# Linear attention and a gated convolution on one core: from four tokens of a head per partition to nine, with all transposes on TensorE and a new instruction list

## The chip, the core and the metric

The kernel runs on one core of a Trainium2 chip. The metric is the device time of one execution, in microseconds (us). Three executions of the kernel before took 235.14, 232.63 and 233.62 us, median 233.62.

## The reference

Two stages follow each other, for 8 batches of 576 tokens. The first is an attention without softmax over pairs, with 8 heads of 64 columns and 128 projected features:

```python
def phi(x):                                   # q and k alike
    proj = np.einsum('bhsd,df->bhsf', x, w_phi)
    proj = proj - np.max(np.abs(proj), axis=-1, keepdims=True)
    return np.concatenate([np.exp(proj), np.exp(-proj)], axis=-1)
kv  = np.einsum('bhsf,bhsd->bhfd', k_p, v)
num = np.einsum('bhsf,bhfd->bhsd', q_p, kv)
den = np.einsum('bhsf,bhf->bhs', q_p, z)[..., None] + 1e-06   # z: sum of k_p over the tokens
```

`num / den`, its heads side by side, is x (576 x 512 per batch). The second stage is a gated layer: `gate[s] = sigmoid(sum over k of conv_w[k] * x[s-4+k])`, five taps of its own for each of the 512 columns, then `(gate * (x @ w_val)) @ w_out`.

## The kernel before

**Units.** A partition holds four tokens that follow each other of each head, so 128 partitions hold 512 tokens of a head. The 64 tokens that are left over in each batch are a "tail". A pair of batches is worked off in nine units of 1024 rows each: one tail unit (two batches, eight heads, 64 tokens) and eight main units (one batch and one pair of heads each). There are 36 units. The head pair lies in the two halves of TensorE's rows.

**One unit, in the names of the instruction list.** `LD` loads and casts to bf16 (GpSimd's DMA queue). `T` transposes k and q on TensorE (L331: 8 whole-array transposes into one PSUM bank), `Tc` copies the bank to SBUF (L224 on VectorE, L222 on ScalarE). `PK` and `PQA` project with tokens on the partitions (L342: pairs of 64-row matmuls of 128 columns, one in each row half), only the largest absolute value of each row is wanted of the q one. `mKa`, `mK`, `mQa`, `mQ` are these row maxima on VectorE (L356, 128x512 each). `K0` to `K3` are the exponentials of k on ScalarE (L388, 128x512), `E` those of the maxima. k's shift is not subtracted but multiplied into v: `V` on GpSimd (L408, L412). `KV` sums over tokens (L445: 16 matmuls of 65 columns, and L450: 4 more for the tail's tokens, with zeroed rows for the other batch). `KVM` copies that sum to SBUF. `PQ` projects q a second time with the features on the partitions (L466: 2 matmuls of 512 columns), `SH` subtracts q's maxima in PSUM (L476: 8 whole-array matmuls of 128 columns, the maxima broadcast as the stationary operand, a negative identity as the moving one). `Qa`, `Q` are the exponentials of q (L484, four of 128x512). `NUM` multiplies with the k-v sum (L509; L523 for the tail), `XN` divides (L534, L536).

**From x to the output.** `XP` puts x's columns on the partitions, by DMA transposes that SyncE issues (L545 for the main tokens, L548 for tails) into `XT` and `XH`; `HL` copies a halo of four tokens. `GA` is the convolution: for each of five taps a diagonal matrix times shifted columns (L604: the array in four tiles of 64x64, 32 matmuls in one `GA`, two `GA` per batch). `TH` is the gate's tanh on ScalarE (L612, 128x1024), `VA` the value product (L617, 16 matmuls of 512 columns per batch), `GV` gate times value (L633), `OUT` the last product (L642), `OE` its copy (L649 on ScalarE, L651 on VectorE), `ST` the store (SyncE). `GAt` to `STt` do the same for tails (L673, L681, L704, L716).

**Order.** `ORDER` is one written list of these names. A number behind a name is the unit or the batch tile, `@` names PSUM banks, and the letter behind the colon an engine. The engines get their instructions in the list's order and wait for each other by semaphores. PSUM is eight banks of 512 float32 columns, allotted by the list. `GA`, `VA` and `OUT` of a batch stand between the attention ops of later batches.

Of the kernel before, what the change touches and what calls it, by code (L numbers as in the profile page):

```python
# [2 lines left out]

# [7 lines left out]
ALU = mybir.AluOpType  # L11
# [9 lines left out]
SM = 512  # L21
ST = S - SM
E1 = D + 1
PL = 144
TL = 80
NG = B // 2
NU = 9 * NG


# [3 lines left out]
LD7 LD6 CK0 CQ0 T1@1 LD2 ND0:A W20 Tc1:D PK1@2,5 mKa1 PQA1@6,1 K01 mK1 mQa1 mQ1 T0@0 LD0 Tc0:A  # L33
PQ1@3,4 PK0@7,6 K11 K21 mKa0 T2@0 E1 Tc2:D K31 K00 SH1 Qa1 LD1 PK2@1,0 mK0 mKa2 LD3 mK2 PQA2@3,5
mQa2 ZV0:P LD8 K20 mQ2 T3@2 E0 Tc3:D PQA0@3,5 mQa0 mQ0 K02 K10 K30 E2 K22 PK3@7,6 mKa3 PQA3@2,5
LD4 mQa3 Q1 LD9 PQ2@3,4 SH2 LD10 mK3 K32 K12 T4@0 Tc4:D PK4@1,0 K03 Qa2 mQ3 V0:P K23 V1:P KV1@3 Q2
LD5 V2:P mKa4 K33 K04 KVM1:D NUM1@4 PQ3@6,3 SH3 mK4 XN1 LD11 K13 KV2@2 K24 LD31 PQA4@7,4 KVM2:D E3
mQa4 K14 mQ4 PQ0@1,5 K34 SH0 LD30 Qa3 Qa0 NUM2@6 PQ4@2,0 T5@4 T6@1 Q3 SH4 Q0 XN2 Qa4 E4 Tc5:D
Tc6:D PK5@7,6 mKa5 K05 PQA5@3,1 PK6@2,5 mQa5 Q4 LD13 K15 mK5 LD12 V3:P K25 KV3@3 mQ5 V4:P mKa6 K06
LC0 K35 KVM3:D E5 V5:P LD32 LD39 PQ5@0,1 TP0@7 mK6 Vb0:P NUM3@3 CW0 XP1 XN3 K16 XP2 T7@7 Tc7:D K26  # L40
SH5 Qa5 PQA6@6,2 mQa6 PK7@3,7 mKa7 KV4@4 PQA7@6,0 mQ6 mQa7 XP3 K36 T8@5 Tc8:D mK7 PQ6@2,6 Q5
KVM4:A SH6 K07 NUM4@4 mQ7 XN4 E6 PK8@0,1 K17 mKa8 Qa6 K27 T9@2 Tc9:D Q6 XP4 PQA8@3,5 V6:P PQ7@4,6
SH7 mQa8 LD15 mK8 K08 K37 PQA9@2,3 mQ8 mQa9 KV5@7 KVM5:D mQ9 T10@5 Tc10:D K18 PQ8@0,2 SH8 Qa7
PK9@4,7 mKa9 T11@3 E7 V7:P Q7 PK10@5,6 Tc11:D K28 mKa10 LD14 DG0:P Qa8 K38 KV6@3 Q8 K09 NUM5@0 mK9
KVM6:D NUM6@2 XN5 K010 mK10 KV7@0 K29 K110 XN6 K19 KVM7:D T12@5 PK11@1,4 mKa11 K210 HL0:P Tc12:D
XP6 LD16 K39 GA0@2 K310 mK11 K011 NUM7@6 VAa1@0 LD40 XN7 E8 VAb1 TH0 GV1 V8:P PK12@2,5 PQA10@3,6
K111 PQ9@1,7 SH9 VAa2@0 K211 mQa10 mKa12 LD19 VAa0@3 mK12 E9 LD17 K311 Qa9 VAb0 mQ10 KV8@4 KVM8:D
VAb2 GV0 PQA11@1,6 K012 V9:P Q9 mQa11 K212 PQ10@4,7 SH10 mQ11 K112 T13@3 Tc13:D NUM8@1 XN8 E10
# [54 lines left out]

class _U:
    pass

@with_exitstack
def kernel(  # L110
# [30 lines left out]

    PS = psum.tile([P, 8, 512], FP32, name="PS")


    units = []
    for G in range(NG):
        for kind in range(9):
# [616 lines left out]
```

## Time and profile before

| | |
|---|---|
| three executions | 235.14, 232.63, 233.62 us, median 233.62 |
| span of the profiled execution | 232.5 us, 8372 instructions |
| that execution's own time | not recorded apart from its span; the median of the runs is 1.1 us above the span |
| busy: TensorE, VectorE, ScalarE, GpSimd | 205.8, 184.2, 188.6, 125.4 us |
| first matmul, first gate matmul, last matmul's end | 4.8, 56.1, 227.7 us |
| DMA | 62002 packets, 30.90 MB |

PE is TensorE's matmuls, PEld its weight loads (they overlap), DVE VectorE, ACT ScalarE, POOL GpSimd, SP SyncE. "Busy" counts from an instruction's start to its recorded end. Matmuls, and also instructions of the other engines, overlap their successors, so a share of the chain of work says better what an instruction costs in a sequence than its duration does.

### The profile page before, as it was taken

Reading aid. Unit: us, or ns where it says so; the run is one execution under the profiler, and the core shown is the slowest. Engines: PE = TensorE matmul, PEld = TensorE weight load, DVE = VectorE, ACT = ScalarE, POOL = GpSimd, SP = SyncE. Lnnn points to the kernel's source line nnn. Section 1 sums busy time; section 2 is a strip of 40 time slices with the busy share of each in tenths; the row PEclk is TensorE's granted clock in tenths of the full one; section 3 lists DMA queues with packets and bytes.
Section 4 is the critical chain, followed back from the end, with each engine's and each line's share of the span. In section 5 each row is a group of like instructions: output and inputs, shape, how many; then the busy total and the mean of one; then the engine's idle time right before and its main releaser. Section 6 shows DMA issues by size and latency. Waiting matters only on the chain.

```text
span 232.5 us, 8372 instructions
## 1 busy us (share of the span) xinstructions
PE 205.8 (89%) x3497; PEld 139.5 (60%) x3516; DVE 184.2 (79%) x335; ACT 188.6 (81%) x419; POOL 125.4 (54%) x142
## 2 busy tenths in 40 slices
PE   1286797888999989899999999999899999999991
PEld 1264675666666746567666766766476667564550
DVE  5559669999989979699999879897799788554451
ACT  3189869999997988599999979998899999934251
POOL 8909935999979437774919751564526241100000
PEclk9998579999999999999999999999999999999997
DMA  8997995979999942999994992499903928126195
GB/s 151 246 198 97 106 180 80 92 101 178 129 194 128 139 32 32 129 257 177 128 114 68 180 186 92 39 115 126 214 6 37 169 77 259 38 52 200 27 355 185
DMA packets 62002, 30.90 MB, mean 133 GB/s; under 512 B 33420, under 2 KB 59148, under 8 KB 61964
## 3 DMA queue, kind: packets, MB, share of 16 engines
q0 software_dynamic: 36144, 14.29, 58.2%
q1 hardware_dynamic: 25468, 15.78, 33.6%
q8 instruction: 27, 0.44, 0.8%
q10 hardware_dynamic: 352, 0.30, 0.4%
q14 instruction: 11, 0.09, 0.2%
HBM read 30.48 MB, written 9.44 MB: 172 GB/s over the span
## 4 chain that ended last, share of the span: by engine, by line
PE 69%; ACT 11%; DMA 9%; DVE 5%; issue 3%; SPq 1%; POOL 1%; POOLq 0%; DVEq 0%; ACTq 0%
PE PS L617 11%; PE PS L642 10%; PE PS L342 7%; PE PS L604 7%; PE PS L476 7%; PE PS L445 6%; PE PS L331 6%; DMA XT<-XN 6%; PE PS L509 5%; ACT QTIL L484 5%; ACT KTIL L388 3%; DMA kT<-in_k_dram 3%; PE PS L466 3%; PE PS L681 2%; DVE MQ L356 2%
## 5 line engine op out<-in xcount | busy, mean ns | idle before, releaser
L408 POOL TENSOR_TENSOR VT<-vN,E 128x1024 bf16<-128x1024 bf16 x27 | 51.5, 1907 | 60.4 <-issue 34.2
L388 ACT ACTIVATE KTIL<-PS 128x512 bf16<-128x512 f32 x128 | 76.7, 666 | 5.3 <-DVE MK L356 5.1
L484 ACT ACTIVATE QTIL<-PS 128x512 bf16<-128x512 f32 x128 | 71.0, 666 | 2.5 <-PE PS L476 1.1
L356 DVE TENSOR_REDUCE MK<-PS 128x4 f32<-128x512 f32 x72 | 47.9, 683 | 7.5 <-PE PS L342 7.2
L356 DVE TENSOR_REDUCE MQ<-PS 128x4 bf16<-128x512 f32 x72 | 47.4, 683 | 1.3 <-PE PS L342 1.2
L342 PE MATMUL PS<-W,T 64*128 64x128 bf16 x576 | 29.6, 227 | 5.8 <-DVE T L224 1.9
L617 PE MATMUL PS<-XT,WVAL 128*128 128x512 bf16 x128 | 33.8, 380 | 0.3 <-DMA XT<-XN 0.3
L342 PEld LDWEIGHTS <-T 64*128 64x128 bf16 x576 | 18.3, 98 | 21.8 <-issue 11.9
L642 PE MATMUL PS<-WOUT,GV 128*128 128x512 bf16 x111 | 29.9, 380 | 1.2 <-issue 0.5
L633 DVE SCALAR_TENSOR_TENSOR GV<-GATE,PS 128x512 bf16<-128x512 bf16 x32 | 21.6, 681 | 5.9 <-ACT GATE L612 3.1
L445 PE MATMUL PS<-VT,KTIL 128*128 128x65 bf16 x512 | 25.4, 198 | 0.8 <-DVE T L224 0.6
L536 DVE TENSOR_TENSOR XN<-PS,RCP 128x512 bf16<-128x512 f32 x36 | 24.9, 691 | 1.2
L445 PEld LDWEIGHTS <-KTIL 128*128 128x128 bf16 x512 | 22.8, 100 | 3.7 <-DVE T L224 0.8
L476 PE MATMUL PS<-nident,MQ 128*128 128x128 bf16 x288 | 23.9, 229 | 0.5 <-issue 0.5
L612 ACT ACTIVATE GATE<-PS 128x1024 bf16<-128x1024 f32 x16 | 16.7, 1044 | 8.8 <-PE PS L604 8.7
L476 PEld LDWEIGHTS <-MQ 128*128 128x128 bf16 x288 | 17.6, 102 | 9.5 <-issue 8.8
L224 DVE COPY T<-PS 128x1024 bf16<-128x1024 bf16 x31 | 21.1, 684 | 2.7 <-PE PS L331 2.3
L509 PEld LDWEIGHTS <-QTIL 128*128 128x128 bf16 x512 | 19.3, 99 | 5.5 <-DVE KVS L224 1.1
L509 PE MATMUL PS<-KVS,QTIL 128*128 128x65 bf16 x512 | 21.4, 196 | 1.3 <-DVE KVS L224 0.8
L450 PE MATMUL PS<-VZ,KTt 128*128 128x65 bf16 x128 | 21.9, 196 | 0.0
L604 PE MATMUL PS<-XT,DIAG 64*64 64x384 bf16 (+3 forms) x512 | 20.6, 299 | 1.0 <-issue 0.8
L642 PEld LDWEIGHTS <-GV 128*128 128x128 bf16 x128 | 11.3, 98 | 12.4 <-issue 0.6
(73 smaller groups left out, 304.1 us busy)
## 6 DMA issues: line engine op xcount, KB each, us to landing
out_dram<-OS SPq DMA_DIRECT2D x14, 512.0 KB, 3.8
kN<-in_k_dram POOLq DMA_DIRECT2D x7, 512.0 KB, 9.0
qN<-in_q_dram POOLq DMA_DIRECT2D x7, 512.0 KB, 8.4
vN<-in_v_dram POOLq DMA_DIRECT2D x7, 512.0 KB, 6.9
vF<-in_v_dram SPq DMA_DIRECT2D x2, 512.0 KB, 7.6
out_dram<-OSt SPq DMA_DIRECT2D x8, 128.0 KB, 2.4
out_dram<-OS SPq DMA_DIRECT2D x4, 256.0 KB, 2.9
qT<-in_q_dram POOLq DMA_DIRECT2D x8, 64.0 KB, 5.2
```

The source lines that it names most:

```text
L342: nc.tensor.matmul(PS[:, bank[rg], blk * P:(blk + 1) * P], u.T[r, i, blk, :], W2[r, :], start=True, stop=True,)
L356: nc.vector.tensor_reduce(dst, PS[:, bank, :].rearrange("p (b f) -> p b f", f=F), AX.X, ALU.max, apply_absolute_value=True,)
L388: nc.scalar.activation(u.KT[:, ft, rg, :, :].rearrange("p b f -> p (b f)"), PS[:, u.PK[rg], :], AF.Exp, scale=1.0 if ft == 0 else -1.0,)
L408: eng.tensor_tensor(dst[:, :, :, 0:D], x.unsqueeze(1).to_broadcast([n, 2, 8, D]), e.unsqueeze(3).to_broadcast([n, 2, 8, D]), ALU.mult,)
L445: nc.tensor.matmul(o, u.KT[:, ft, rg, h2 * 2 + j2, :], u.VT[:, ft, (h2 * 2 + j2) * 2 + rg, :], start=(c == 0), stop=False,)
L476: nc.tensor.matmul(PS[:, u.PQ[rg], blk * P:(blk + 1) * P], u.MQ[:, rg, blk:blk + 1].to_broadcast([P, P]), nident[:, :], start=False, stop= ...
L484: nc.scalar.activation(u.QT[:, ft, rg, :, :].rearrange("p b t -> p (b t)"), PS[:, u.PQ[rg], :], AF.Exp, scale=1.0 if ft == 0 else -1.0,)
L509: nc.tensor.matmul(ps[:, j2, x * E1:(x + 1) * E1], u.QT[:, ft, rg, h2 * 2 + j2, :], u.KVS[:, (ft * 2 + h2) * E1:(ft * 2 + h2 + 1) * E1], s ...
L536: nc.vector.tensor_tensor(u.XN[:, :, :, :], nv[:, :, :, 0:D], RCP[:, :, :].unsqueeze(3).to_broadcast([P, 2, 4, D]), ALU.mult,)
L604: nc.tensor.matmul(ps[c, par, j0 * P:j1 * P], DIAG[r, dt, 4 - dl, :], mv, start=(i == 0), stop=(i == len(parts) - 1), skip_group_check=True,)
L617: nc.tensor.matmul(PS[:, m.val[jt], :], WVAL[:, dt, jt * P:(jt + 1) * P], XTs[m.b % 2][:, dt, :, 16:PL], start=(dt == 0), stop=(dt == 3),)
L642: nc.tensor.matmul(PS[:, bank[0], :], m.GV[:, jt, j * P:(j + 1) * P], WOUT[:, jt, :], start=(jt == 0), stop=(jt == 3),)
```

## The change

The layout, the list and nearly every function are new. What is computed, and the types, are as before.

- **Layout.** 576 = 64 x 9: a partition holds nine tokens that follow each other, and a head fills 64 partitions, so a pair of heads fills 128. Token n of each partition is "plane" n. A unit is planes 0 to 7 of one head pair of one batch (1024 rows, 32 units). Plane 8 of a batch's four pairs is a smaller unit of 512 rows, `halos[b]` in the code (its ops end in `e`; 8 of them). There is no tail, no `XH` and no `HL`: the four tokens ahead of a partition's first token are planes 5 to 8, one partition column to the left. The loads read 2304 bytes in one piece where they read 1024 (256 for tails).
- **Transposes.** `XP` is four TensorE transposes into PSUM (L545 of the new kernel; L694 for plane 8), and `XC` copies them to `XT`, on VectorE or ScalarE. No DMA transposes remain. `Te` transposes plane 8 in 64x64 tiles (L572).
- **KV sums.** The two heads lie in different row halves: 36 matmuls of 64 rows, 65 columns, in pairs, one in each row half and each with its own PSUM bank (L431).
- **q's second projection and shift.** `PQa` (each row half into the bank of the other head) and `PQb` (into its own) are two matmuls of 256 columns each (L466). `PQb` may start when `PQa` has ended: SyncE waits for `PQa` and releases TensorE (`WQ`, L458, 40 in all). `SH` is 16 matmuls of 64 rows and 64 columns in pairs (L484).
- **Taps.** `GA` covers a batch: 144 matmuls on 32x32 tiles, sixteen tile positions (L720); `GAe` 80 for plane 8 of two batches (L831). It takes four PSUM banks at once, where it took two.
- **Wider ops.** `mQ` is one reduction over 128x1024 (L333), `Qp` and `Qm` are two exponentials of 128x1024 (L499). k's stay at 128x512.
- **Others.** `WVAL` is reordered by four copies on GpSimd, `NF` = 8 matmuls on zeros run ahead of the first transposes, stores go plane by plane (2 KB pieces), and the pools' depths differ.

The core of the diff (new line numbers are those named above):

```diff
-    def op_KV(i, bank):                       # 20 matmuls, 128 rows
-        u.KVps = PS[:, bank[0], 0:4 * E1]
-        for ft in range(2):
-            for h2 in range(2):
-                for c in range(4):
-                    j2, rg = c // 2, c % 2
-                    nc.tensor.matmul(o, u.KT[:, ft, rg, h2 * 2 + j2, :],
-                        u.VT[:, ft, (h2 * 2 + j2) * 2 + rg, :], start=(c == 0), stop=False)
-                nc.tensor.matmul(o, ut.KT[:, ft, h2, u.hp, :],
-                    VZ[u.G % 2][u.b % 2][:, ft, 2 * u.hp + h2, :], start=False, stop=True)
+        u.KVps = half(bank[0], 2 * E1)        # a bank for each row half
+        for ft in range(2):
+            for n in range(NPL):
+                for h2 in range(2):
+                    r = row(h2)
+                    if n < 8:
+                        kt, vt = u.KT[r, ft, n % 2, n // 2, :], u.VT[r, ft, n, :]
+                    else:
+                        kt, vt = t.KT[r, ft, u.hp % 2, u.hp // 2, :], t.VT[r, ft, u.hp, :]
+                    (nc.tensor.matmul(u.KVps[:, h2, ft * E1:(ft + 1) * E1], kt, vt,
+                        start=(n == 0), stop=(n == 8), skip_group_check=True))
...
-    def op_PQ(i, bank):                       # 2 matmuls of 512 columns
-                PS[:, bank[rg], :], W2[r, :], u.T[r, 1, :, :].rearrange("p b t -> p (b t)"),
+    def relay(u):
+        u.relay = nc.sync.nop()
+        behind(u.relay, u.last)
+    def swapped(proj, u):
+        behind([proj(u, g, 0) for g in range(2)][0], u.relay)
+    def featproj(u, g, swap):
+        h2 = g ^ swap
+        return nc.tensor.matmul(
+            PS[:, u.PQ + h2, :].rearrange("p (j g t) -> p g j t", g=2, t=64)[:, g, :, :],
+            W2[row(g), :], u.T[row(g), 1, :, h2, :], start=True, stop=False, skip_group_check=True)
...
-        for rg in range(2):                   # op_SH
-            for blk in range(4):
-                nc.tensor.matmul(PS[:, u.PQ[rg], blk * P:(blk + 1) * P],
-                    u.MQ[:, rg, blk:blk + 1].to_broadcast([P, P]), nident[:, :], ...)
+        for n, col in enumerate(cols):        # submax: 8 columns of maxima
+            for h2 in range(2):
+                r = row(h2)
+                nc.tensor.matmul(PS[:, bank + h2, n * 64:n * 64 + 64],
+                    col[r, :].to_broadcast([64, P]), nident[r, r], ...)
...
-            nc.sync.dma_start_transpose(XTs[u.b % 2][:, u.hp, :, 16:PL], xf)
+        for n in range(4):                    # op_XP, then op_XC copies u.XP to XT
+            nc.tensor.transpose(u.XP[:, n * P:(n + 1) * P], xf[:, n * P:(n + 1) * P], ident[:, :])
...
-        for i, (dl, j0, j1) in enumerate(parts):          # op_GA, twice per batch
-            for dt, r, c, par in quarters(q2):            # 4 tiles of 64x64
-                nc.tensor.matmul(ps[c, par, j0 * P:j1 * P], DIAG[r, dt, 4 - dl, :], mv, ...)
+        for i, (dl, j0, j1) in enumerate(parts):          # taps, once per batch: 9 parts
+            for dt in range(4):
+                for r in rs:                              # 4 x 4 tiles of 32x32
+                    rr = slice(32 * r, 32 * r + 32)
+                    g = PS[32 * dt:32 * dt + 32, bank[r // 2] + r % 2, j0 * 64:j1 * 64]
+                    nc.tensor.matmul(g, DIAG[rr, dt, 4 - dl, :], mv, ...,
+                        tile_position=(32 * r, 32 * dt))
...
+            u.QT[:, ft, :, :, :].rearrange("p h n t -> p h (n t)"), half(u.PQ, 512),   # qexp
```

Two or three places show how the instructions stand. First TensorE inside one KV sum, in front of the summand of the left-over tokens, before (`KTIL` are k's features of the unit, `KTt` those of the tail, `VZ` the tail's scaled v):

```order
L445 LDWEIGHTS KTIL
L445 MATMUL PS<-VT,KTIL 128x65
L450 LDWEIGHTS KTt
L450 MATMUL PS<-VZ_119,KTt 128x65
L445 LDWEIGHTS KTIL
L445 MATMUL PS<-VT,KTIL 128x65
```

and now, where `KTe` and `VTe` belong to plane 8, and two rows that read alike go to the two row halves:

```order
L431 LDWEIGHTS KT
L431 MATMUL PS<-VT,KT 128x65
L431 LDWEIGHTS KTe
L431 MATMUL PS<-VTe,KTe 128x65 [waits Pool_49]
L431 LDWEIGHTS KTe
L431 MATMUL PS<-VTe,KTe 128x65
```

The matmuls keep their 65 columns; one on 128 rows has become two on 64 rows each. Second, TensorE at the second projection of q and the shift behind it, before:

```order
L342 MATMUL PS<-W_134,T 128x128
L466 LDWEIGHTS W_134
L466 MATMUL PS<-T,W_134 128x512
L466 LDWEIGHTS W_134
L466 MATMUL PS<-T,W_134 128x512 [waits Activation_49]
L476 LDWEIGHTS MQ
L476 MATMUL PS<-nident,MQ 128x128
```

and now, in unit 2, one of the places where nothing stands between `PQa` and `PQb`:

```order
L466 LDWEIGHTS W_116
L466 MATMUL PS<-T,W_116 128x4x64 [waits DVE_49]
L466 LDWEIGHTS W_116
L466 MATMUL PS<-T,W_116 128x4x64
L466 LDWEIGHTS W_116 [waits SP_sequencer_49]
L466 MATMUL PS<-T,W_116 128x4x64
L466 LDWEIGHTS W_116
L466 MATMUL PS<-T,W_116 128x4x64
L484 LDWEIGHTS MQ
L484 MATMUL PS<-nident,MQ 128x64
```

The projection has become four matmuls with a wait for SyncE in the middle, and everything behind it on TensorE stands behind that wait. In 31 of the 40 places at least 0.4 us of other matmuls (by their columns) have been put between the two halves by the list; in five places there is nothing. Third, VectorE where a unit's result leaves, before:

```order
L224 CAST KVS<-PS 128x260 [waits PE_49]
L534 RECIPROCAL RCP<-PS 128x8 [waits PE_49,Activation_49]
L536 TENSOR_TENSOR XN<-PS,RCP 128x512 [waits DVE_49]
L356 TENSOR_REDUCE MK<-PS 128x4
L534 RECIPROCAL RCP<-PS 128x8 [waits PE_49,Activation_49]
L536 TENSOR_TENSOR XN<-PS,RCP 128x512 [waits DMAHW4_49,DVE_49]
```

and now:

```order
L333 TENSOR_REDUCE MQ<-PS 128x8 [waits PE_49,Activation_49]
L777 SCALAR_TENSOR_TENSOR GV<-GATE,PS 128x512 [waits PE_49]
L143 COPY XT_112<-PS 128x512 [waits PE_49]
L530 RECIPROCAL RCP<-PS 128x8 [waits PE_49]
L535 TENSOR_TENSOR XN<-PS,RCP 128x512 [waits DVE_49]
L143 CAST KVS<-PS 128x260 [waits PE_49,Activation_49]
```

The copy `XT<-PS` has come in, the wait of `XN` for a DMA has gone, and `MQ` is one instruction for both halves (128x8 where it was twice 128x4).

1034 lines of the change are left out of this document (579 added, 455 removed), and 14 rows, old and new, of the table LOADS.

## The prediction

> **What bounds the kernel now.** First the head of the page: how busy each engine is, and when.
>
> ```profile
> span 232.5 us, 8372 instructions
> ## 1 busy us (share of the span) xinstructions
> PE 205.8 (89%) x3497; PEld 139.5 (60%) x3516; DVE 184.2 (79%) x335; ACT 188.6 (81%) x419; POOL 125.4 (54%) x142
> PE   1286797888999989899999999999899999999991
> DVE  5559669999989979699999879897799788554451
> ACT  3189869999997988599999979998899999934251
> PE 69%; ACT 11%; DMA 9%; DVE 5%; issue 3%; SPq 1%; POOL 1%; POOLq 0%; DVEq 0%; ACTq 0%
> ```
>
> TensorE (PE) is the busiest engine and holds 69% of the chain of work that ended last. But the digits show two regimes: in the first ten slices (58 us) PE has gaps while VectorE and ScalarE are full, later PE is full, and in the last five slices VectorE and ScalarE run dry. The windows view gives the three stretches (PE, PEld, DVE, ACT, POOL busy us, then PE's granted clock):
>
> ```profile
> 0.00:55.00 55.00, 38.71 (x594) 29.15 (x595) 42.15 (x78) 42.65 (x99) 41.13 (x52) 0.91 1.08 141
> 55.00:200.00 145.00, 140.07 (x2540) 95.25 (x2557) 128.92 (x233) 133.50 (x303) 84.31 (x91) 1.00 0.98 127
> 200.00:232.50 32.50, 27.01 (x375) 15.12 (x368) 13.09 (x26) 12.43 (x21) 0.00 (x0) 0.96 0.47 147
> ```
>
> From 55 to 200 us PE is busy 97% of the time, ScalarE 92%, VectorE 89%. So after the first gate matmul every microsecond taken from PE's stream should come off the end, as long as ScalarE and VectorE, 8 points behind, don't become the bound. Four rows of the chain, in order of time (start, us, what), mark the ends of the stretches and a trap:
>
> ```profile
> 3.83 7.29 DMA kT<-in_k_dram
> 56.08 1.22 PE PS L604 x32
> 71.66 9.28 DMA XT<-XN
> 227.76 0.69 DVE OS L651
> ```
>
> The second unit's data land at 11.1 us (3.83 + 7.29). The first gate stands at 56.1. After 227.7 only a copy and the store are left, 4.7 us. The DMA transposes (`XT<-XN`) look expensive, yet the group of the matmuls that read them says what PE really lost there: 0.3 us before the value matmuls (the number behind the second bar is idle time and its cause).
>
> ```profile
> L617 PE MATMUL PS<-XT,WVAL 128*128 128x512 bf16 x128 | 33.8, 380 | 0.3 <-DMA XT<-XN 0.3
> ```
>
> So I give the removal of the DMA transposes nothing by itself; it also takes their wait off `XN`.
>
> **The change part by part: TensorE.** Durations are no use here, since matmuls overlap (a value matmul "lasts" 380 ns). The chain counts each piece from its start to the next one's:
>
> ```profile
> 57.89 0.86 PE PS L617 x4
> 63.15 0.55 PE PS L476 x8
> 63.70 0.45 PE PS L331 x8
> 96.42 0.69 PE PS L673 x40
> 118.61 0.63 PE PS L523 x32
> 125.57 0.55 PE PS L342 x16
> ```
>
> A whole-array matmul of 512 columns takes 0.86/4 = 0.215 us, one of 128 columns 0.45/8 = 0.056. The shift (`L476 x8`, 128 columns too) shows 0.55, because it comes behind another tiling of the array: 0.10 per change of tiling. `L342 x16` is 8 pairs of 64-row matmuls, 0.55 - 0.10 = 0.45: 0.056 per **pair**, so the two row halves run at once. `L523 x32`, 16 pairs in column halves of 65 columns: (0.63 - 0.10)/16 = 0.033 per pair. `L604 x32` above is four tiles at once: 1.22 for 32 matmuls of 320 columns on average, which one after the other would take over 4. Now each edit, at these prices:
>
> - `SH`: 36 x 0.45 = 16.2 before. Now 288 pairs of 64 columns at 0.033 = 9.6: **-6.6**.
> - `GA`: 16 x (1.22 - 0.10) = 17.9 before. Now 9 parts per batch with 16 tiles each. With all 16 at once a part costs its columns (512, 448, 64, 384, 128, 320, 192, 256, 256 at 0.215 per 512, the 64 at the 0.056 of 128): 1.1 per batch, 8.9: **-9.0**. `GAe`: 4 x (0.69 - 0.10) = 2.4 before, now 20 groups of 128 columns, 1.1: **-1.3**.
> - KV: two rows of the timeline (start, us) bound one of the 20-matmul sums, from 70.77 to the next unit's matmul at 71.49:
>
> ```profile
> 70.77 0.29 PE L445 MATMUL PS<-VT,KTIL 128*128 128x65 bf16 x4
> 71.49 0.40 PE L342 MATMUL PS<-W,T 64*128 64x128 bf16 x8
> ```
>
>   0.72 - 0.10 = 0.62 per unit, 32 x 0.62 = 19.8. Now 18 pairs at 0.033, 576 pairs: 19.2, **-0.6**.
> - New transposes of x: 144 x 0.056 = **+8.1**. `T`: four units fewer, -1.8; `Te` 32 groups of four 64-column tiles at 0.033, +1.1.
> - Changes of tiling: I count 161 in the new list against 165: -0.4. `PQ` has the same columns. The 8 matmuls on zeros run before any data are there.
>
> Sum: -6.6 - 9.0 - 1.3 - 0.6 + 8.1 - 0.7 - 0.4 = **-10.5 us**.
>
> **The unknown prices in it.** The trace has no pair on row halves of under 128 columns and no 32x32 tile. For the 65-column pair the nearest row is `L523`, 0.033; but its weights are 64 columns wide, and the new ones 128. If the two weight loads of a pair took turns, 64 columns would cost at most 0.0165 and 128 at most 0.033, and the pair 0.066. So KV plus SH lie between 28.8 and 57.6. I take 0.033, because `L342`'s pairs, whose weights are 128 wide, show no sign of turns at 0.056. For the 32x32 tiles the low end is 1.1 per batch. `L673 x40` gives (0.69 - 0.10)/40 = 15 ns per matmul as the fastest issue over a long row; at that, 144 take 2.1, and `GA` 17.0 instead of 8.9 (+8.1). I take the low end, since the quads of `L604` do follow their columns.
>
> The Trainium skill ("TensorE: Matmul & The Clock Gate", Measured speedup vs the span model) tells of a speedup of 10.6, not 16, for sixteen 32x32 tiles. By that `GA` would cost 1.7 per batch, an estimate from that page, and the sum would be 4.5 us worse; no run here shows it yet.
>
> **The wait between `PQa` and `PQb`.** PE must wait until `PQa` has ended and SyncE has passed it on; SH and all that follows on PE stands behind.
>
> ```profile
> L466 PE MATMUL PS<-T,W 64*128 64x512 bf16 x72 | 15.5, 399 | 0.9 <-ACT QTIL L484 0.8
> 61.86 0.19 PE L450 MATMUL PS<-VZ,KTt 128*128 128x65 bf16 x1
> 62.16 0.43 DVE L224 CAST KVS<-PS 128x260 bf16<-128x260 f32 x1 [0.22 <-PE PS L450]
> L604 PEldq EVENT_SEMAPHORE  x1: 51/51/51, 55.6 to 55.6; - x1
> ```
>
> A 512-column matmul ends 399 ns after its start, 0.18 us after its columns are through; a hand-over takes 62.16 - 61.86 - 0.19 = 0.11; waiting alone 0.05. So `PQa`'s end, two hand-overs and SyncE: 0.18 + 0.22 + 0.05 = 0.45 us. In 31 of 40 places the list puts 0.4 us or more in between: nothing. Of the nine others four stand bare in the first stretch, where PE waits anyway. The other five (0, 0.22, 0.3, 0.3, 0.37 us of cover) cost together 1.1: **+1**. Were all 40 bare, 18 us. SyncE's own queue adds stores ahead of two of the 40; they wait for copies issued long before.
>
> **ScalarE and VectorE.** Instructions in a row again cost less than they last (first two rows: ScalarE in sequence; then single ones):
>
> ```profile
> 45.22 1.37 ACT L484 ACTIVATE QTIL<-PS 128x512 bf16<-128x512 f32 x2
> 46.17 1.89 ACT L388 ACTIVATE KTIL<-PS 128x512 bf16<-128x512 f32 x3
> 47.60 1.43 ACT L484 ACTIVATE QTIL<-PS 128x512 bf16<-128x512 f32 x2
> 69.65 0.60 ACT L388 ACTIVATE KTIL<-PS 128x512 bf16<-128x512 f32 x1
> 73.16 1.02 ACT L612 ACTIVATE GATE<-PS 128x1024 bf16<-128x1024 f32 x1 [1.26 <-PE PS L604]
> 17.65 1.28 DVE L356 TENSOR_REDUCE MQ<-PS 128x4 bf16<-128x512 f32 x2
> 18.85 0.68 DVE L224 COPY T<-PS 128x1024 bf16<-128x1024 bf16 x1
> 19.45 1.28 DVE L356 TENSOR_REDUCE MQ<-PS 128x4 bf16<-128x512 f32 x2
> ```
>
> ScalarE: 512 columns cost (47.60 - 46.17)/3 = 0.48 in a row, 1024 cost 1.02 - 0.60 = 0.42 more, 0.90. q's exponentials: 144 x 0.48 = 69 before, 64 x 0.90 + 16 x 0.48 = 65 now, -4. New on it: 14 `XC` copies (ten of 512), +6; four more output copies, +2; the rest +1. **+5**. VectorE: 512 float32 cost (18.85 - 17.65)/2 = 0.60, the 1024 bf16 of `T` 19.45 - 18.85 = 0.60. A maximum over 1024 then costs about 1.13 (512 more at 0.53): 32 x 1.13 + 8 x 0.60 = 41 against 72 x 0.60 = 43. 22 `XC` of 512 bf16 are half of `T`'s slope, 0.34: +7.5, four small ones and eight `Te` +3.5. Four output copies, two `T` and four `KVS` go to other engines or away, -5; two memsets and one `VT` go, -3. **+1**. GpSimd, 54% busy, has four units less of VT and stays out.
>
> So PE gives 10.5 and ScalarE takes 5: the distance between them from 55 to 200 us, 140 against 133.5 busy, all but closes. The two still fit side by side, for ScalarE ran at 100% where it was the bound (the nines from slice 7).
>
> **Start.** 1.9 MB must land ahead of the second unit (both first pairs in float32, then k and q of batch 1 and one pair more of batch 0), and the page's first two slices of 5.8 us moved 2.3 MB:
>
> ```profile
> GB/s 151 246 198 97 106 180 80 92 101 178 129 194 128 139 32 32 129 257 177 128 114 68 180 186 92 39 115 126 214 6 37 169 77 259 38 52 200 27 355 185
> ```
>
> That is 10 us, like the 11.1 now. Ahead of the first gate the new list has as many exponentials and maxima as the old. I cost the start at 0, between -6 and +4.
>
> **The sum.** 232.5 - 10.5 + 1 = 223 of span, and 1.1 to the median of the runs (the profiled execution's time is known by its span alone): **224 us**.
>
> **The rivals.**
> - *The bound passes to ScalarE and VectorE.* Half of PE's gain comes back as waits for PSUM banks; `GA`'s four banks at once and KV's second one speak for it, the 8 points of slack against it: 229.
> - *More is gained.* The first gate comes earlier, since larger pieces load faster and 54% busy GpSimd is freed: up to 6 us, 218.
> - *Slower: the weight loads of a row-half pair take turns.* Place: KV and SH. Price 57.6 - 28.8 = 29 us, all on PE: 253. It decides from 9.5 us on, at 864 pairs 11 ns each: a pair at 0.044 in place of 0.033. For it: the trace has never loaded two 128-wide weights in less than 0.056. Against: `L523` and `L604` keep tiles in step.
> - *Slower: each small matmul has a floor of its own.* At the 20 ns that `L523` shows per matmul (0.63/32), 144 taps cost 2.9 a batch (+14), `GAe` +5, KV +4, SH +2: 249. `L673`'s 15 ns speaks against it. The Trainium skill ("TensorE: Matmul & The Clock Gate", Back-to-back issue gap) puts such a floor at about 25 ns for 1 to 64 columns, which as an estimate from that page would make it over 260; `L523`, at 20 ns with its change of tiling, is already under it.
> - *It doesn't do what it says:* PE's stream is shorter, but a wait for loads, stores or SyncE takes its place: 234.
>
> **How the numbers follow.** Forecast 224: 0.45. More gained, 218: 0.15. Passed bound, 229: 0.2, a third of it inside 1% of 233.6. Taking turns, 253: 0.1. Floor, 249: 0.05. Replaced wait, 234: 0.05. 1%, 2.3 us, is about what three runs that spread over 2.5 us can tell from no change. Faster by over 1%: 0.45 + 0.15 + 0.13 = 0.73; within: 0.07 + 0.04 = 0.11; slower: 0.16. The range reaches from 211 (both the -6 of the start and some stalls gone) to 238 (the 8 us of slow taps on 229) and leaves out the two slow cases and some tail.
>
> **What would show it.** In the new profile PE's `SH` should stand at about 0.27 us for its 16 matmuls, a KV sum at 0.60 for 36, `GA` at 1.2 to 1.3 for 144; the first gate near 56 us; ScalarE and VectorE within some points of PE in the middle. The forecast is wrong if KV pairs start 0.05 us apart or more, if taps start 15 ns apart all along, if PE waits long for SyncE, or if the first gate moves by more than 5 us.

## The result: 250 us where 224 was forecast, and the profile after

| | before | after |
|---|---|---|
| four executions, median (range) | 233.88 us (232.63 to 235.14) | 250.1 us (248.26 to 251.59) |
| ratio after/before, 95% interval | | 1.0705 (1.0629 to 1.0781) |
| profiled execution: its time, its span | span 232.5 us | 250.12 us, span 248.3 us |
| first gate matmul, last matmul's start | 56.1, 227.3 us | 57.0, 242.2 us |

The change made the kernel 7% slower. In all tables a ratio leaves out executions that lie over 1.5% above the fastest of their kernel, so it can differ a little from the ratio of the medians, and it is left blank where too few executions remain.

The start went as forecast: the first gate stands at 57.0 us. All the loss lies behind it. First lines of the page of the kernel after that answer to those of before (engines, slices of 6.2 us, the instruction queue, shares of the chain):

```profile
span 248.3 us, 12153 instructions
PE 212.1 (85%) x5452; PEld 147.9 (60%) x5452; DVE 185.9 (75%) x327; ACT 193.7 (78%) x385; POOL 102.0 (41%) x124
PE   5577878787979599699995899898998999999990
DVE  1559898996866479569983799788986999686450
ACT  2559989997678479849994899798998999996320
q8 instruction: 42, 0.69, 1.1%
PE 61%; DVE 13%; issue 9%; ACT 9%; DMA 4%; SPq 1%; POOL 1%; DVEq 0%; POOLq 0%
```

PE's busy time rose, its share fell. The digits no longer show a full PE behind the tenth slice: 5, 6 and 7 stand between the nines, and ScalarE and VectorE dip with it. The chain names what is new: **issue**, time in which PE waited for nothing that the profile shows, 9% where it was 3%. The stretches that the prediction used, again (PE, PEld, DVE, ACT, POOL, then PE's clock):

```profile
0.00:55.00 55.00, 40.83 (x932) 31.61 (x933) 41.24 (x72) 43.17 (x89) 35.89 (x52) 0.81 0.85 150
55.00:200.00 145.00, 128.97 (x3480) 88.50 (x3479) 113.93 (x201) 119.45 (x240) 56.61 (x63) 0.98 0.51 95
200.00:248.30 48.30, 42.34 (x1052) 27.76 (x1046) 30.71 (x57) 31.05 (x59) 9.53 (x10) 0.98 0.37 90
```

In the 145 us in the middle PE is busy 129 (89%) where it was 140 (97%), and neither VectorE (79%) nor ScalarE (82%) has become the bound. The chain in order of time (start, us, what) shows how the holes look:

```profile
59.45 0.55 PE PS L304 x8
60.12 0.65 PE PS L756 x3
60.77 1.74 issue
62.51 1.25 PE PS L756 x5
...
69.92 1.75 PE PS L720 x121
71.67 0.54 PE PS L785 x2
72.21 1.68 issue
...
75.80 0.58 PE PS L431 x36
...
80.37 0.80 PE PS L831 x80
...
82.40 0.23 PE PS L484 x16
82.63 0.97 PE PS L756 x4
83.60 2.68 issue
86.28 0.61 PE PS L545 x4
```

At 60.77 PE stops for 1.74 us in the middle of a run of eight value matmuls whose operands are all there. No engine, no DMA and no semaphore of the program releases it. The waits of PE name the same thing for five of its lines (us in total, times, longest):

```profile
PE PS L545 <- issue: 3.5, 2, 2.7
PE PS L316 <- issue: 3.4, 3, 2.2
PE PS L756 <- issue: 3.1, 2, 1.7
PE PS L720 <- issue: 3.0, 4, 1.7
PE PS L785 <- issue: 1.7, 1, 1.7
```

For before the same view has such rows too, but small ones, and its page has a smaller instruction queue:

```profile
PE PS L604 <- issue: 0.8, 1, 0.8
PE PS L476 <- issue: 0.5, 1, 0.5
PE PS L509 <- issue: 0.4, 1, 0.4
```
```profile
q8 instruction: 27, 0.44, 0.8%
```

Queue 8 carries the instructions. 42 transfers with 0.69 MB together are 16 KB each; PE's 10,904 matmuls and weight loads in 42 pieces are some 260 each. Counted along PE's stream (matmuls, weight loads and PE's few semaphore instructions), the long gaps of the kernel after start at number 193 to 195 of every 256, at whichever op the list has there: 11 gaps behind the first gate, 14.9 us together. The three small ones of the kernel before stand at 193 and 194 too. Around the gap at 60.77 the view of the DMA queues, cut to 60.2 to 61.4 us, holds one transfer of that queue (from 59 to 60.2 there is none):

```profile
q0 software_dynamic: 72, 0.06, 33.0%
q8 instruction: 1, 0.02, 5.1%
```

It runs from 60.3 to 61.3 us, and PE goes on at 62.51. So the theory that the experiments had to test, **F**: PE's instructions come in blocks of 256; the next block is asked for when the one before is entered; between entry (the start of number 196, just behind the places of the gaps) and the start of that transfer lie 1.1 us in the median behind the first gate, and over 2 us in six of 35 cases; the transfer takes 0.9 to 1.5; and where PE stood still, it went on 1.2 to 1.6 us behind the transfer's end. (The request itself is not in the trace, so that it comes at the entry is inferred from these times.) A block that PE works off faster than that ends in a gap. Before, the transfers came no sooner (1.7 us in the median, over 2 in ten of 22 cases), but a block lasted at least 5.8 us (7.7 in the median); the new stream, with 2,944 of its instructions on 32x32 tiles alone, has blocks of 1.4 us (5.2 in the median). The rivals: **L**, the new list's hand-offs between engines cost the time; **T**, the weight loads of a row-half pair take turns (already against the trace: a sum of 36 at 0.58 us, `SH` of 16 at 0.23, both above).

### The profile page after: what moved, and what is told of

The parts are those of the page before. It is cut to its first block, busy times and chain, and to the rows that moved or that the text cites. A ratio compares the mean times of both kernels' runs of the same rounds, so it can differ in the third digit from the quotient of the medians.

```text
span 248.3 us, 12153 instructions
## 1 busy us (share of the span) xinstructions
PE 212.1 (85%) x5452; PEld 147.9 (60%) x5452; DVE 185.9 (75%) x327; ACT 193.7 (78%) x385; POOL 102.0 (41%) x124
## 4 chain that ended last, share of the span: by engine, by line
PE 61%; DVE 13%; issue 9%; ACT 9%; DMA 4%; SPq 1%; POOL 1%; DVEq 0%; POOLq 0%
PE PS L756 10%; PE PS L785 9%; PE PS L720 6%; PE PS L431 6%; PE PS L316 6%; PE PS L517 5%; DMA qN<-in_q_dram 4%; PE PS L304 4%; ACT KT L381 3%; DVE MK L333 3%; PE PS L466 3%; PE PS L484 3%; PE PS L545 2%; ACT QT L499 2%; DVE T L143 2%
## 5 line engine op out<-in xcount | busy, mean ns | idle before, releaser
L381 ACT ACTIVATE KT<-PS 128x512 bf16<-128x512 f32 x128 | 68.5, 626 | 6.5 <-PE PS L316 3.7
L499 ACT ACTIVATE QT<-PS 128x1024 bf16<-128x1024 f32 x64 | 62.7, 1040 | 9.9 <-PE PS L484 9.0
L333 DVE TENSOR_REDUCE MK<-PS 128x4 f32<-128x512 f32 x64 | 42.9, 683 | 8.2 <-PE PS L316 6.6
L333 DVE TENSOR_REDUCE MQ<-PS 128x8 bf16<-128x1024 f32 x32 | 38.9, 1219 | 4.5 <-PE PS L316 3.1
L745 ACT ACTIVATE GATE<-PS 128x1024 bf16<-128x1024 f32 x16 | 15.6, 1022 | 12.3 <-PE PS L720 11.4
L431 PE MATMUL PS<-VT,KT 64*128 64x65 bf16 x1024 | 23.8, 194 | 0.5 <-issue 0.2
L517 PE MATMUL PS<-KVS,QT 128*128 128x65 bf16 x512 | 22.6, 198 | 0.9 <-ACT KVS L141 0.9
L517 PEld LDWEIGHTS <-QT 128*128 128x128 bf16 x512 | 20.0, 101 | 4.3 <-ACT QT L499 0.8
L431 PEld LDWEIGHTS <-KT 64*128 64x128 bf16 x1024 | 20.9, 97 | 2.7 <-DVE XT L143 0.4
L466 PE MATMUL PS<-T,W 64*128 64x256 bf16 x128 | 19.2, 291 | 1.5 <-DVE MQ L333 1.1
L720 PE MATMUL PS<-XT,DIAG 32*32 32x126 bf16 (+8 forms) x1152 | 16.5, 285 | 3.0 <-issue 3.0
L720 PEld LDWEIGHTS <-DIAG 32*32 32x32 bf16 x1152 | 12.4, 87 | 7.5 <-issue 5.4
```

The costliest lines, as they stand in the source:

```text
L333: nc.vector.tensor_reduce(dst, x, AX.X, ALU.max, apply_absolute_value=True)
L381: nc.scalar.activation(u.KT[:, ft, par, :, :].rearrange("p b f -> p (b f)"), PS[:, u.PK[par], :], AF.Exp, scale=1.0 if ft == 0 else -1.0,)
L431: (nc.tensor.matmul(u.KVps[:, h2, ft * E1:(ft + 1) * E1], kt, vt, start=(n == 0), stop=(n == 8), skip_group_check=True,))
L466: return nc.tensor.matmul(PS[:, u.PQ + h2, :].rearrange("p (j g t) -> p g j t", g=2, t=64)[:, g, :, :], W2[row(g), :], u.T[row(g), 1, :, h ...
L499: nc.scalar.activation(u.QT[:, ft, :, :, :].rearrange("p h n t -> p h (n t)"), half(u.PQ, 512), AF.Exp, scale=1.0 if ft == 0 else -1.0,)
L517: (nc.tensor.matmul(u.NUM[:, jj // 2, x * E1:(x + 1) * E1], u.QT[:, ft, h2, 2 * jj:2 * jj + 2, :].rearrange("p n t -> p (n t)"), u.KVS[:, ...
```

## The experiments

"Gaps" are my own sum over the profiled execution: every step from one matmul's start to the next behind 57 us that is over 0.15 us longer than its columns at 2.4 per ns (512 in 0.215 us) and 0.1 us, and has no releaser; what counts is the time beyond columns and 0.1 us. The trace of before lacks 19 of its 3,516 matmuls, and three steps across a missing one are left out of its gaps. "PE" is the number of matmuls and weight loads on the page, "blocks" the transfers of queue 8.

| kernel | PE | blocks | gaps, us | median us (range) | ratio to before (95%) |
|---|---|---|---|---|---|
| before | 7,013 | 27 | 1.9 | 233.9 (232.0 to 236.5) | |
| after | 10,904 | 42 | 14.9 | 250.1 (248.3 to 251.6) | 1.071 (1.063 to 1.078) |
| e1_thin | 9,384 | 36 | 9.3 | 244.5 (240.3 to 244.6) | |
| e2_halo | 9,880 | 38 | 6.6 | 242.1 (239.6 to 246.8) | 1.027 (1.018 to 1.036) |
| e3_fewloads | 10,904 | 42 | 6.5 | 243.3 (239.8 to 245.5) | 1.043 (1.034 to 1.052) |
| e7_halo_few | 9,880 | 38 | 0.3 | 232.8 (229.7 to 233.6) | 0.991 (0.985 to 0.996) |
| e4_split | 9,144 | 36 | 5.0 | 241.2 (236.3 to 242.1) | |
| e9_before_few | 7,032 | 27 | 0 | 231.5 (230.1 to 232.5) | 0.990 (0.987 to 0.994) |
| e16_split_few | 9,144 | 36 | 0.3 | 234.5 (233.0 to 236.1) | 0.999 (0.995 to 1.003) |
| e8_shift | 11,032 | 43 | 16.3 | 254.9 (one) | |
| e10_pieces | 10,904 | 42 | 15.2 | 251.6 (251.5 to 255.6) | 1.074 (1.066 to 1.083) |
| e11_halo_pieces | 9,880 | 38 | 4.6 | 238.3 (236.5 to 239.7) | 1.017 (1.008 to 1.026) |

### Fewer instructions, or fewer loads, in the new kernel

**e1_thin** leaves the second row half out of most `KV` and `SH` pairs: the array is busy as long, since the halves run side by side, but 1,520 instructions go.

```diff
-                for h2 in range(2):
+                for h2 in range(2 if n == 0 else 1):     # in KV and in submax
```

> The changed kernel, with 1520 of its 10899 TensorE instructions left out that take next to no array time of their own: of each pair of row-half matmuls in the KV sums and in the shift, the second row half's is issued only once per sum and bank (so the second head's sums and shifts are incomplete). Theory F (TensorE runs out of instructions: each block of 256 is fetched while the one before it runs, and the fetch takes 3 to 6 us): fewer blocks, fewer stalls, 240 to 245 us against 250. Rival L (the new list's hand-overs and PSUM waits): same array time, same waits, 248 to 250. Rival T (the pairs take turns on the array): 235 or less, and the KV matmuls' share falls by half.

244.5 us, gaps 9.3: down by 5.6 us, and as much of it is gap. One of the four executions took 240.3; all of them lie below L's number (248 to 250) and above T's (235).

**e2_halo** computes the same output with taps in 5 parts in place of 9: each partition's four planes ahead of its first token are copied (GpSimd, 128x1008) in front of its planes, so that no part wraps around.

```diff
-    PARTS = [p for dl in range(5) for p in ([(dl, dl, 8), (dl, 0, dl)] if dl else [(0, 0, 8)])]
+    PARTS = [(dl, 0, 8) for dl in range(5)]
+    def op_HX(b, eng):
+        copy(eng, X[:, :, 0:4, 1:64], X[:, :, 9:13, 0:63])
```

> The changed kernel with the taps in 5 parts in place of 9: GpSimd copies planes 5 to 8, one partition column to the right, ahead of plane 0, so each tap is one run of 512 columns. 64 matmuls and 64 weight loads fewer per batch (1024 instructions), the gate's array time from about 1.75 to about 1.2 us. Theory F: 239 to 244 us (4 of array time and some 3 to 7 of stalls). Rival L: 245 to 250 (the array time at most, the copy's wait against it).

242.1 us, in F's range and below L's, though one of the four executions (246.8) reaches into L's. This edit mixes two savings: undisturbed, a batch's taps also fall from 1.75 us to 1.28 (from their first matmul to the next op's), 4 us in all, and the copy brings waits of its own (`PE <- POOL XT`, 1.7 us). The gaps fell by 8.3.

**e3_fewloads** leaves PE's instructions as they are and takes the loads of batches 3 to 7 away; batch 2's tiles stand in.

```diff
     def tok(name, b):
+        b = min(b, 2)
     def load(eng, name, b, p0, p1):
+        if b > 2:
+            return
```

> The changed kernel with the loads of k, q and v for batches 3 to 7 left out (these batches compute on batch 2's data). The instructions of TensorE stay what they are; the DMA engines are idle but for stores and instruction fetches. Theory F, with the fetch held up behind loads: the delay from entering a block to its fetch falls from up to 3.9 us to about 1, the stalls mostly go, 236 to 244 us. Theory F without that (the fetch is slow by itself): 248 to 250 with the same stalls. Rival L: 248 to 251, since nothing waited for these loads.

243.3 us, gaps 6.5, with the same 42 blocks. The transfers themselves take as long as ever (median 0.98 us against 0.97); what shortens is the time from a block's entry to the start of the transfer: 0.7 us in the median for 1.1, and none of 35 is over 2 us (the longest 1.7), where six were. So data transfers hold up the instructions'.

**e7_halo_few** does both.

> The new kernel with taps in 5 parts and the loads of batches 3 to 7 left out (batch 2's tiles stand in, so their values are not computed). Each alone took about 7 us off. Theory F: they cut the same stalls, one by fewer blocks and one by earlier fetches, so less than the sum of both: 236 to 239 us, unexplained PE gaps 4 to 6 us. Rival S (two separate causes, the shorter taps and the loads' own delay): the full sum, 235 us or less, with gaps as in each alone.

232.8 us. F's number (236 to 239) is missed, since I had thought that the two would share one saving; the rival has the time right and the gaps wrong, for they did not stay. Both cuts work on one distance, a block's time against its transfer's delay, and together they close it. Behind the first gate the gaps are all but gone (0.3 us), and one of 31 transfers starts over 2 us behind its block's entry, where e2_halo has ten of 32. Most of what the waits still show as "issue" lies ahead of the gate:

```profile
PE PS L662 <- POOL XT L79: 1.3, 3, 0.7
PE PS L611 <- DVE XN L477: 0.7, 1, 0.7
PE PS L258 <- issue: 0.6, 1, 0.6
```
```profile
55.00:200.00 145.00, 140.70 (x3573) 96.47 (x3566) 129.70 (x232) 135.98 (x275) 61.03 (x65) 1.00 0.18 45
```

PE is busy 97% of the middle again, at clock 1.00, as before the change.

### The same two causes on the kernel before

**e4_split** adds 2,112 instructions to the kernel before: value and output products in four matmuls of 128 columns (0.056 us each for 0.217, so about 2 us of array time more), `SH` in two of 64.

```diff
+            for s in range(4):
                 nc.tensor.matmul(
-                    PS[:, m.val[jt], :], WVAL[...], XTs[m.b % 2][:, dt, :, 16:PL],
+                    PS[:, m.val[jt], s * P:(s + 1) * P], WVAL[...], XTs[m.b % 2][:, dt, s, 16:PL],
```

> The kernel before, with the value and output matmuls in four pieces of 128 columns and the shift in two of 64: 2112 TensorE instructions more (9139 in place of 7027), about 2 us more of array time (the 512 columns cost 4 x 56 in place of 216 ns). Theory F: stalls at block ends appear, 238 to 244 us against 233.9. Rival L: 235 to 236, the array time alone.

**e9_before_few** takes the loads of batches 3 to 7 away from the kernel before.

```diff
+        if kind == "m" and n > 2:
+            main[name, n] = main[name, 2]
+            return
         if kind == "m":
```

> The kernel before, in which batches 3 to 7 reuse the loaded main tiles of batch 2 (their loads are left out, so their values are not computed). It is the control for the same cut in the new kernel, which took 250 us to 243. Theory F (PE waits for its own instructions, whose fetches queue behind the loads): PE of the kernel before loses only 1.9 us in gaps without a releaser, so 232 to 234 us, at most 2 us below the kernel before. Rival D (loads delay data or hold the array back in either kernel): the same 7 us come off here, 227 us.

**e16_split_few** does both.

> The kernel before with value and output products in four matmuls of 128 columns and SH in two of 64 (2112 PE instructions more, about 2 us of array time), and with batches 3 to 7 on batch 2's loaded main tiles (their loads left out, their values not computed). Each alone gave 241.2 and 231.5 us. Theory F, both causes needed: the added stall goes with the loads, 233 to 236 us, gaps at block entries under 1.5 us. If instructions cost on their own (the sequencer): 238 to 239 us.

The medians make a square: 233.9 us, 241.2 with more instructions, 231.5 with fewer loads, 234.5 with both. Without the loads 2,112 instructions cost 3.0 us (ten executions each), of which some 2 are columns. What they cost with the loads is less certain: three of e4's four executions took 241.2 to 242.1 us, the fourth 236.3, which is about what rival L allows. So the times alone don't settle the square. The profiled executions support F, e4's being one of the long ones (242.1): gaps of 1.9, 5.0, 0 and 0.3 us, all of them at 193 or 194, and transfers that start over 2 us behind their block's entry in ten of 22 cases, nine of 31, none of 22 and one of 31. Rival D (loads alone cost 7 us in either kernel) is out. A fixed price per instruction (238 to 239 for both edits, worked out from e4's 241) missed e16; from 236.3 it would not have, but it would not gather gaps at 193. e16 lies in F's range and e9 0.5 us below it.

### Where the gaps stand, and the size of the loads

**e8_shift** runs 64 matmuls of 8 columns on zeros ahead of everything, 128 instructions that cost no time themselves.

```diff
+    for i in range(64):
+        nc.tensor.matmul(PS[:, 7, 0:8], zero[:, 0:P], zero[:, 0:8], start=True, stop=True)
```

> The new kernel with 64 matmuls of 8 columns on zeros ahead of the first transposes: 128 PE instructions more before any data are there, so every later instruction has an index 128 higher. Theory F (fetch by blocks of 256 instructions): the gaps without a releaser stand again at index 193 to 195 of a block, so at other places of the program, 128 instructions earlier; which of them are long changes, the time stays at 246 to 254 us. Rival L (places in the list, hand-offs): the gaps stay at the same places of the program, so at index 66 of a block.

The gaps moved to other places and kept their number in the block: all nine without a releaser that are over 0.8 us start at 193 to 195. L has them at 66, where none is. Its chain near the first gate (the gap is now inside the taps, where it was among the value matmuls):

```profile
58.29 1.35 PE PS L722 x71
59.65 2.50 issue
62.15 1.09 PE PS L722 x45
```

The same program with a shifted grid took 254.9 us in its one execution, 0.9 over F's range, with gaps of 16.3 us. That their length depends on which ops a block happens to hold is likely and not shown.

**e10_pieces** splits each load of 576 KB (batches 3 to 7) into four of 144, spread over the list.

> The new kernel with the loads of batches 3 to 7 in four pieces of 144 KB each (one head pair), spread over the list 14 names apart, instead of one of 576 KB. Same bytes, same PE instructions. Theory F with fetches that queue behind the load in flight: the queue in front of a fetch gets shorter, 243 to 247 us, gaps without a releaser 8 to 12 us in sum. If it is the sum of the traffic that delays a fetch: 249 to 251 us, gaps 15 us as before.

No change: 251.6 us, gaps 15.2, and again six of 35 transfers start over 2 us behind their block's entry. The size of a single load is not what delays an instruction transfer. That less traffic helps and smaller pieces do not leaves open where they queue.

### The transposes of x, put back on DMA

**e5_xbar** undoes one part of the change; **e6_halo_xbar** does the same on e2_halo.

```diff
-XP4@2 ... XC4:D          # 32 times in the list
+XC4                      # nc.sync.dma_start_transpose, as the kernel before
```

> The new kernel with the main units' x transposed by DMA again (SyncE), as the kernel before does: 128 transposes and 32 copies less, 256 PE instructions less (one fetch block). Theory F with my prices: 128 x 0.056 = 7.2 us of array time and about 1 us of stall off PE, unless the DMA transposes make the fetches later: 241 to 244 us. Rival L (the list's hand-offs set the end, and x comes 9 us later through the DMA): 248 to 252 us.

> The new kernel with taps in 5 parts over planes with a copied halo (1024 PE instructions less) and x transposed by DMA: 1280 PE instructions less in all. Theory F: 242 (taps alone) less 8, 233 to 236 us, about the kernel before, with PE gaps without a releaser at 6 to 9 us in sum. Rival L: 241 to 245 us.

276.9 (271.1 to 279.3) and 281.2 us (277.0 to 287.4): all forecasts missed, by 25 to 45 us. The waits of PE in e5_xbar name it:

```profile
PE PS L655 <- DMA XT<-XN: 18.1, 10, 5.9
PE PS L401 <- SPq L393: 3.1, 2, 1.8
```

The new list puts the taps right behind the copy of x. A DMA transpose there comes up to 5.9 us late, and the next `PQb` waits for SyncE, which now stands in a queue of transposes. I read this as no price of DMA transposes as such: the op was put back without a list made for it. No run here gives it such a list. That the kernel before lost next to nothing by its transposes rests on its own profile (0.3 us before the value matmuls), not on these runs.

### Towards a faster version

**e11_halo_pieces**: e2_halo with the loads in pieces and the halo copied head pair by head pair on GpSimd (128x189 each, right behind each `XC`).

> The new kernel with taps in 5 parts (halo copied per head pair on GpSimd, 1024 PE instructions less) and the loads in pieces. Theory F: 236 to 241 us, gaps without a releaser 4 to 8 us. If pieces do nothing: 241 to 243 us.

238.3 us, in F's range and the fastest on the new layout with nothing left out, still 1.7% slower than before. Since pieces alone did nothing in e10, the copies may have done it; these runs do not tell. **e12_diag** takes 896 more instructions out: `SH` as one matmul of 512 columns per row half, on a diagonal of the maxima that GpSimd builds, and `SH` later in the list.

```diff
-                nc.tensor.matmul(PS[:, bank + h2, n * 64:n * 64 + 64], col[r, :].to_broadcast([64, P]), nident[r, r], ...)
+            nc.tensor.matmul(PS[:, u.PQ + h2, :], ones[row(h2), :], u.DQ[row(h2), :, :].rearrange("p n t -> p (n t)"), ...)
```

> The kernel of the run before (taps in 5 parts, loads in pieces) with the shift SH of a main unit as one matmul of 512 columns in each row half, on a diagonal of the maxima that GpSimd builds, and SH later in the list: 896 PE instructions less, so 1920 less than the new kernel; about 0.05 us of array time less per unit. Theory F: 231 to 236 us, gaps without a releaser 2 to 5 us. Rival: GpSimd's product (about 1 us per unit) and its place in GpSimd's queue make SH late, 240 us or more, with PE waiting for POOL.

287.7 us: the rival's side, far beyond its price and not by its sign, for PE waited 1.0 us for the diagonal. In the waits ScalarE stands for `SH`, and GpSimd's queue for the maxima:

```profile
ACT QT L468 <- PE PS L457: 51.5, 25, 8.4
POOL DQ L448 <- DVE MQ L289: 40.7, 14, 13.0
```

Two edits were mixed there, so three runs took them apart. **e13_halo_spread** is e2_halo with the copies per head pair, 11 on GpSimd and 29 on VectorE; **e14_diag_dve** adds the diagonal on VectorE with `SH` where it stood; **e15_diag_dve_late** moves `SH` to just ahead of the exponentials.

> The new kernel with taps in 5 parts over planes with a copied halo; the halo copies go per head pair, on GpSimd where x is early and on VectorE right behind x's own copy where the taps follow soon. 1024 PE instructions less than the new kernel; loads as there. Theory F: 235 to 239 us, gaps without a releaser at block entries 4 to 7 us, no wait of PE for POOL before the taps. If the copies on VectorE (25 of about 0.25 us) hold the maxima back: 240 to 243 us.

> e13_halo_spread with the shift SH of a main unit as one matmul of 512 columns in each row half on a diagonal of the maxima, which VectorE builds right behind the maxima; SH stands where it stood. 896 PE instructions less than e13_halo_spread, 32 products of 128x512 bf16 more on VectorE (0.35 to 0.6 us each). Theory F: 2 to 3 us less stall per 1000 instructions, so 233 to 236 us. Rival: VectorE is late by 0.5 us at every SH, 240 to 250 us. If e12_diag's 288 us came from SH itself and not from GpSimd: 270 us or more.

> As e14_diag_dve, with SH moved in the list to just ahead of q's first exponential, as e12_diag had it. If e12_diag's loss came from the late SH (ScalarE's exponentials wait for it): 260 us or more, with ACT waiting 40 us for SH. If it came from GpSimd's queue: within 5 us of e14_diag_dve.

250.3, 270.5 and 287.2 us (ratios 1.067, 1.153 and 1.221), gaps 6.1, 2.2 and 0.6. e13 and e14 miss F's numbers; e14 ends where its last alternative has it (270 us or more), e15 where its first has it (260 or more). The gaps fell and the time rose; a longer execution also leaves each transfer more time, so these runs are no clean test of F. e13's waits show what the forecast had too low: PE now waits for `XN` (`PE <- DVE XN`, rows of 2.0, 1.6, 1.0 and 0.4 us), since VectorE, in the list's order, stands for x's copies on ScalarE and for GpSimd (below). e15 against e14 puts 17 us on the later place of `SH` (ScalarE waits 48.6 us for it, against 11.4), and e14 against e13 puts 20 on the diagonal on VectorE, 32 products that take 31.5 us of its queue. How much of e12's loss was GpSimd's queue and how much the late `SH` stays open, since e12 and e15 end within 1 us of each other. No version here beats the kernel before.

## Why the prediction was wrong

**The step that failed: "Sum: -10.5 us".** It priced PE by columns and never by the number of instructions. The stretch from the first gate to the last matmul (in e2_halo and e7_halo_few, whose first gates stand at 62.9 and 59.1 us, from 57 us on), taken step by step from one matmul's start to the next (gaps as in the table, "waits" those with a releaser):

| us | all | work | gaps | waits |
|---|---|---|---|---|
| before | 171.3 | 166.7 | 1.9 | 2.7 |
| after | 185.2 | 168.7 | 14.9 | 1.7 |
| e2_halo | 178.1 | 166.8 | 6.6 | 4.7 |
| e7_halo_few | 167.9 | 163.1 | 0.3 | 4.5 |

Of the 26 us by which the forecast was low, 13.0 are gaps (14.9 - 1.9). Most of the other half is `work`: it rose by 2.0 us where the sum had it fall by 10.5. The profile of before had the sign: 27 transfers of instructions, three bare gaps of 0.4 to 0.8 us, "issue 3%" in the chain, which I quoted and did not ask about; and the order said that PE's rows grow from some 7,000 to 10,900. A term was called for: blocks of 256 at the new pitch, against the time from a block's entry until PE could go on in the next one, in the kernel before 4 us in the median and up to 8 (an estimate: the transfer's end in the trace and some 1.3 us).

The Trainium skill ("Runtime: NRT & Kernel Launch", Instruction fetch mechanics) says that instructions are fetched in blocks of 256 by a queue of the sequencer's own, and that crossing a block is "mostly hidden". The 256 agree with the gaps at 193 to 195 of every 256; the hiding does not hold here, with gaps of up to 2.7 us and 14.9 in sum, and the runs decide.

**The taps, mis-sized.** A batch's `GA` was put at 1.1 us and a change of tiling, 1.2; the chain has 1.75 (69.92 above). `GAe` was put at 0.375 (1.1/4 and a change); the chain has 0.80. Together 8 x 0.55 + 4 x 0.42 = 6.1 us. The prediction let a short part cost as little as its columns. Long parts do: those of 512, 448 and 384 columns take 0.226, 0.190 and 0.162 us, so sixteen 32x32 tiles run at once, and in e2_halo, where all five parts have 512 columns, each of the first four takes 0.215 to 0.227 (the rest of the 1.28 us is the last part and the change of tiling):

```profile
206.62 1.28 PE PS L659 x80
```

Short parts have a floor: those of 63, 126 and 189 columns take 0.185, 0.183 and 0.173 us in `GA` where 0.056 to 0.08 was put, and in `GAe` 128 columns take 0.133 where 0.056 was put, so 8 to 12 ns per matmul. The price lies between the two ends that the prediction gave (1.1 and 2.1 us a batch). The 1.7 that it worked out from the 10.6 of the Trainium skill (TensorE: Matmul & The Clock Gate, Measured speedup vs the span model) is close to 1.75, but that is luck: by the page's 10.6 e2_halo's long parts would take 0.32 us (an estimate from the page), and they take 0.215; the excess lies in the short parts.

**The rest.** Counted by lines behind the first gate, without gaps and waits, the 12.5 us that `work` came out above the sum are 6.8 of taps, 2.5 of value and output products, 1.6 of `SH` and 1.6 of others. The products should have stayed the same; the granted clock in the middle, 0.98 for 1.00, can explain part of that (at most 2.6 us over all 129 busy us). `SH` saved 5.0 us and not 6.6 there: the sum took all units, but 72 of the 288 `SH` matmuls of before stand ahead of the first gate, where the prediction itself had PE waiting. The gate came 0.9 us later, the end behind the last matmul's start took 0.9 longer, the execution lies 1.8 us around its span, not 1.1, and the waits came out at 1.7 us where 2.7 + 1 was forecast. Sum 13.0 + 12.5 + 0.9 + 0.9 + 0.7 - 2.0 = 26.0 of 26; the cause of the products' part and of the last 1.6 stays open.

**What held.** `SH` in 0.23 us for 16 (0.27 forecast), a `KV` sum in 0.58 for 36 (0.60), the first gate at 57, the wait between `PQa` and `PQb` (0.4 us of PE's steps behind the gate, +1 forecast), ScalarE and VectorE under the bound. With the gaps out (e7, which also has the cheaper taps) PE is full again in the middle, but the time is 1% below before where 4% was forecast: the sum in columns was too good as well.

**The rivals.** Weight loads in turns (253) and a floor of 20 ns for every small matmul (249) come close in number and are wrong in mechanism: pairs take 0.029 to 0.033 us, and only the short parts of the taps show a floor, 8 to 12 ns per matmul. The last one, "a wait for loads, stores or SyncE takes its place", was right in kind, but the wait is for the instructions themselves, and I had given it 5% and no price beyond the gain.

## What to carry to other kernels

Count the instructions of the bounding engine as well as its columns: where a rewrite splits matmuls, divide the stream into blocks of 256 and compare each block's time with what a transfer of instructions takes under the kernel's own DMA load (here, from a block's entry until PE can go on in the next, an estimated 3.5 us in the median and up to 6); a burst of small tiles is where it bites. In a profile, look for idle time of the bounding engine that nothing releases ("issue"), and see whether it returns at the same number in a block. Do not expect to undo or move a part of a scheduled kernel alone: transposes, diagonals and copies that looked cheap by their own time cost 8 to 39 us in a list that was not made for them.

## What the runs showed of the hardware

**Instructions compete with data.** Same instructions, fewer loads: gaps from 14.9 to 6.5 us (e3), from 6.6 to 0.3 (e7), from 5.0 to 0.3 (e16). Transfers of instructions that start over 2 us behind their block's entry: from six of 35 to none (e3), from ten of 32 to one of 31 (e7), from ten of 22 to none (e9). Smaller loads of the same sum changed nothing (e10).

**VectorE waits for GpSimd, inside an instruction.** A copy in SBUF (128x252 bf16) takes 0.226 us alone. In e13 one took 1.94, and the timelines of the two engines show why:

```profile
157.69 1.94 DVE L79 COPY XT<-XT 128x252 bf16<-128x252 bf16 x1
159.55 0.41 DVE L79 CAST KVS<-PS 128x260 bf16<-128x260 f32 x1
```
```profile
157.65 1.90 POOL L345 TENSOR_TENSOR VT<-vN,E 128x1024 bf16<-128x1024 bf16 x1 [3.77 <-PE PS L423]
```

It began 0.04 us behind GpSimd's product and ended 0.08 us behind it. Four of the 29 copies took over 0.5 us; all four ran beside such a product and ended 0.08 to 0.09 us behind it. e14's diagonals show the same in their spread, 691 ns alone and up to 2334:

```profile
L439 DVE TENSOR_TENSOR DQ<-ni,MQ x32: 691/693/2334, 10.6 to 243.5; 128x512 bf16<-128x512 bf16 x32
```

The Trainium skill ("SBUF — State Buffer", SBUF: two separate sides) has GpSimd and certain kinds of VectorE instruction share a pair of SBUF ports, as an exclusive lock for the whole instruction; these rows agree. The new kernel's frequent VectorE ops all read PSUM; copies and products within SBUF came in with my edits, and with them this wait.
